# One v transfer cut over Sync and GpSimd, 45 repeated transposes, and three fewer product repeats, in an attention and spectral-mix kernel bound by its weight stream

## The chip, the cores and the metric

One core of one Trainium2 chip. The metric is device time in microseconds (us) of that core; lower is better. The kernel before took 436.51 us (median of 3 runs, 436.29 to 437.32). Every kernel was timed in five rounds against the kernel before on the same chip, and compared by ratios with 95% intervals.

## The reference, cut to what matters

```python
# q, k, v: (8, 8, 576, 64) float32, f: (8, 8, 576)
scores = scale * np.matmul(q, k.transpose(0, 1, 3, 2))
scores = np.where(causal, -1e9, scores + decay)        # decay from cumsum(log f)
attn_out = np.matmul(softmax(scores), v)
x = attn_out.transpose(0, 2, 1, 3).reshape(8, 576, 512)

X = np.fft.rfft(x, axis=1)[:, :64]                     # 64 modes
Yr = einsum('bmd,mde->bme', Xr, w_r) - einsum('bmd,mde->bme', Xi, w_i)
Yi = einsum('bmd,mde->bme', Xr, w_i) + einsum('bmd,mde->bme', Xi, w_r)
y = np.fft.irfft(Y, n=576, axis=1)
u = x + y
out = u + np.maximum(u @ w_ch, 0)
```

The weights w_r and w_i are 64 x 512 x 512 float32 each, 134 MB together. They have to be read once, and this is what most of the time goes to.

## The kernel before

Weights stream through a ring of nine tiles, issued by GpSimd and cast to bf16 on the way; q, k and v of 16 pairs of heads are loaded among them in the same queue. TensorE does attention and multiplies whatever weight tiles have come. After the attention only weight tiles remain, and the last one is handled in four small groups.

```python
    def pool_dma(dst, src):
        keep(nc.gpsimd.dma_start(dst, src))          # program order is kept
    ...
                # loads of pair pr: k, q, v; 128 partitions x 2 x 576 floats
                if nm == "v" and pr < 1:
                    nc.sync.dma_start(dst, ap)
                else:
                    pool_dma(dst, ap)
    ...
        def emit_vback(s):                           # v back to rows, one per step s
            ...
            for sc in range(NSB):                    # five blocks
                nc.tensor.transpose(
                    vp[:, sc, :, :].rearrange("p b d -> p (b d)"),
                    VTs[s // 2 % 2][:, h, sc * 128 : (sc + 1) * 128],
                    ident_bf[:, :],
                )
    ...
        def fill(n):     # products of the tail done again
            for k in range(n):
                rows = slice(k % 2, k % 2 + 1)
                run(*(terms(jobs[0], ps, t, "x")[rows] for t in range(2)), pin=True)

        fill(4)
        emit_modes(nmode)                            # last tile but one
        fill(3)
        emit_modes(nmode + 1, lambda mi, hf: fill((3, 3, 3, 1)[2 * mi + hf]))
```

The softmax here doesn't subtract the row's maximum and nothing guards it: scores larger than these inputs give would overflow.

Of the kernel before, what the change touches and what calls it, by code (L numbers as in the profile page):

```python
# [15 lines left out]
def _strided(ap: bass.AP, free_dims, offset_elems: int = 0) -> bass.AP:  # L16
    new_ap = [list(ap.ap[0])] + [list(x) for x in free_dims]
    return bass.AP(tensor=ap.tensor, offset=ap.offset + offset_elems, ap=new_ap)
# [3 lines left out]
def kernel(  # L22
# [11 lines left out]
    nc = tc.nc  # L34
    B, H, S, Dh = q.shape
# [4 lines left out]
    NSB = 5  # L40
# [14 lines left out]
    NR = S // RP  # L55
    RG = ((0, 5), (5, 4))
    NRING = 9
    STG = 3

    const = ctx.enter_context(tc.tile_pool(name="const", bufs=1))  # L60
    xpool = ctx.enter_context(tc.tile_pool(name="xpool", bufs=1))
# [30 lines left out]
    def pool_dma(dst, src):  # L92
        keep(nc.gpsimd.dma_start(dst, src))  # L93
# [116 lines left out]
    def stage(i):  # L210
        if i != 1:
            return {
                nm: stq.tile(
                    [128, 2, NR, Dh], F32 if nm == "v" else BF16, name=f"st{nm}{i}"
                )
                for nm in "kqv"
            }
        n = 2 * NR * Dh
        flat = {
            "k": wx[:, 0:n],  # L220
            "q": wx[:, n : 2 * n],
            "v": wx[:, 2 * n : 4 * n].bitcast(F32),
        }
        return {
            nm: t.rearrange("p (b r d) -> p b r d", b=2, r=NR)
            for nm, t in flat.items()
        }

    with ExitStack() as actx:
# [25 lines left out]
        NE = 2  # L255
        QKVst = [stage(i) for i in range(STG)]
        VTs = [kt.tile([128, 2, SP], BF16, name=f"VT{i}") for i in range(2)]
# [6 lines left out]
        def emit_loads(pr):  # L264
            dc, bp, _ = steps[2 * pr]
            for nm, src in (("k", k), ("q", q), ("v", v)):
                one = src[2 * bp, 2 * dc, :, :]
                dst = QKVst[pr % STG][nm][:, :, :, :].rearrange("p b r d -> p b (r d)")
                ap = bass.AP(
                    tensor=one.tensor,  # L270
                    offset=one.offset,
                    ap=[[NR * Dh, 128], [H * S * Dh, 2], [1, NR * Dh]],
                )
                if nm == "v" and pr < 1:
                    nc.sync.dma_start(dst, ap)
                else:
                    pool_dma(dst, ap)

# [2 lines left out]
        def emit_transposes(pr, what):  # L281
            dc, bp, _ = steps[2 * pr]
            for which in what:
                st = QKVst[pr % STG][which]
                if which == "q":
# [6 lines left out]
                else:  # L292
# [8 lines left out]
                    )  # L301
                if pr < STG:
                    tc.keep_in_program_order(ins)
# [26 lines left out]
        def scratch(parts, *dims):  # L330
# [13 lines left out]
        ft = ftf[:BH, :]  # L344
        nc.sync.dma_start(ft[:], f.rearrange("b h s -> (b h) s"))
        emit_loads(0)
        nc.gpsimd.memset(trimask[:, :], 1.0)
        nc.gpsimd.affine_select(
# [3 lines left out]
            fill=0.0,  # L352
# [8 lines left out]
            fill=0.0,  # L361
            base=0,
            pattern=[[1, 128]],
            channel_multiplier=-1,
        )
        emit_loads(1)
        emit_w_load(0)
        emit_w_load(1)
# [167 lines left out]
        def emit_vback(s):  # L536
            dc, bp, h = steps[s]
            c0 = 2 * bp * H + 2 * dc + h
            vp = psT.tile([128, NSB, 2, Dh], BF16, tag="tr", name="vp")
            for sc in range(NSB):  # L540
                nc.tensor.transpose(  # L541
                    vp[:, sc, :, :].rearrange("p b d -> p (b d)"),
                    VTs[s // 2 % 2][:, h, sc * 128 : (sc + 1) * 128],
                    ident_bf[:, :],
                )
            va = vap.tile([128, NSB, 2, Dh + 1], BF16, tag="va", name="va")
            nc.vector.tensor_copy(va[:, :, :, 0:Dh], vp[:, :, :, :])
            nc.vector.tensor_copy(
                va[:, :, :, Dh : Dh + 1],
                _strided(wdec[:, 0, c0 : c0 + 1], [[BH, NSB], [H, 2], [1, 1]]),  # L550
            )
            vaugs[s] = va
# [163 lines left out]
        for s in range(NS + 1):  # L716
            pr, h = s // 2, s % 2
            if s == 0:
                emit_loads(STG - 1)
            if h == 1 and pr + STG < NPR:  # L720
                emit_loads(pr + STG)
# [23 lines left out]
            if s < NS:  # L745
                emit_scores(s, 3)
                emit_vback(s)
# [7 lines left out]
    with ExitStack() as bctx:  # L755
# [219 lines left out]
        def terms(job, ps, t, what):  # L975
            rows = [[] for _ in range(2 * len(job))]
            for tt, i, o, hs, src, basis, ysrc in pieces(job):
                if tt != t:
                    continue
                p = ps[t][o, i, :]  # L980
                r = 0 if wide(job) else 2 * i
                rows[r].append((p, ident_bf[hs, hs], src, True))
                rows[r + 1].append((p, basis, ysrc, False))
            return [r for k, r in enumerate(rows) if r and "xy"[k % 2] in what]

        def run(*lists, pin=False):
            for k in range(max(len(l) for l in lists)):
                for l in lists:
                    for a in l[k] if k < len(l) else ():
                        ins = add(*a)  # L990
                        if pin:
                            tc.keep_in_program_order(ins)
# [59 lines left out]
        def fill(n):  # L1052
            for k in range(n):
                rows = slice(k % 2, k % 2 + 1)
                run(*(terms(jobs[0], ps, t, "x")[rows] for t in range(2)), pin=True)

        fill(4)
        emit_modes(nmode)
        fill(3)
        emit_modes(  # L1060
            nmode + 1,
            lambda mi, hf: fill((3, 3, 3, 1)[2 * mi + hf]),
# [83 lines left out]
```

## Time and profile before

| | before |
|---|---|
| time, median | 436.51 us |
| span of the profiled execution | 435.2 us |
| TensorE (PE) busy | 368.1 us, 85% |
| granted TensorE clock, mean | 0.824 |
| last weight landing | 400.19 us |
| from there to the end | 35.0 us |

The page of the kernel before adds two rows, busy tenths over 40 slices of the span:

```profile
PEclk9996899996558665586565869589999999989997
DMA  8999999999999999999999999999999999995797
```

The first is TensorE's granted clock: in the attention stages (from about 100 to 285 us, the 10th to the 26th digit) it is often near one half. The second is the DMA engines: full up to the 36th digit, which ends at 391.7 us; the last weights land in the slice after it.

Several numbers below come from counting the records of the trace rather than from a view. The sorted times of a weight transfer's 16 landings show how far the DMA engines have drifted apart ("stagger"). What bounds a weight tile is the sixteenth.

### The profile page before, as it was taken

How to read it: one execution, taken by the hardware profiler on the slowest of the kernel's cores; microseconds unless marked ns; L12 is line 12 of the kernel's file. 1: busy time of each engine (PE TensorE's matmuls, PEld its weight loads, DVE VectorE, ACT ScalarE, POOL GpSimd, SP SyncE). 2: the span in 40 equal slices, each digit the busy share in tenths (PEclk: the TensorE clock that was granted, in tenths of full speed). 3: DMA queues.
4: the chain of work that ended last, by engine and by line, in shares of the span. 5: the costliest groups of instructions: out<-in, count | busy, mean ns of one | idle time of the engine just before them, and what ended most of it. 6: DMA issues, size and time to landing. Idle time of an engine off the chain costs nothing.

```text
span 435.2 us, 12314 instructions
## 1 busy us (share of the span) xinstructions
PE 368.1 (85%) x5313; PEld 249.7 (57%) x5313; DVE 263.7 (61%) x659; ACT 224.4 (52%) x339; POOL 126.8 (29%) x198
## 2 busy tenths in 40 slices
PE   3787799999987879778787788799999998899881
PEld 2454566776666666566565666656665555454540
DVE  5797888876555655555557568533332665553892
ACT  2887488774526454365462646134434443631781
POOL 8333332333233233232333222223223223200400
PEclk9996899996558665586565869589999999989997
DMA  8999999999999999999999999999999999995797
GB/s 184 234 235 241 234 236 238 235 212 236 234 215 236 225 224 237 210 238 233 214 237 211 212 211 212 211 211 211 211 211 211 212 210 211 211 211 100 253 367 274
DMA packets 50982, 97.38 MB, mean 224 GB/s; under 512 B 3792, under 2 KB 12976, under 8 KB 50928
## 3 DMA queue, kind: packets, MB, share of 16 engines
q0 software_dynamic: 46560, 86.09, 100.9%
q1 hardware_dynamic: 4368, 10.51, 6.7%
q8 instruction: 41, 0.67, 0.6%
q14 instruction: 13, 0.11, 0.1%
HBM read 163.73 MB, written 9.44 MB: 398 GB/s over the span
## 4 chain that ended last, share of the span: by engine, by line
PE 35%; DMA 26%; ACT 12%; DVE 10%; issue 4%; SPq 0%; DVEq 0%; POOL 0%; ACTq 0%
DMA wb<-in_moe_w_i_dram 25%; ACT E L576 8%; PE pav L614 7%; PE ps L569 7%; PE A L188 6%; PE tp L307 5%; PE px L657 2%; PE vp L541 2%; DVE QTs L322 2%; ACT KT L320 2%; ACT VT L326 2%; DVE XT L671 1%; DVE os L1005 1%; DVE E L591 1%; PE px L682 1%
## 5 line engine op out<-in xcount | busy, mean ns | idle before, releaser
L576 ACT ACTIVATE E<-ps 128x1024 bf16<-128x1024 f32 (+1 forms) x128 | 101.5, 851 | 26.1 <-PE ps L569 15.4
L93 POOL DMA_DIRECT2D wb<-in_moe_w_r_dram x64 | 42.5, 664 | 128.9 <-PE A L188 25.1
L188 PE MATMUL A<-XT,wb 128*128 128x16 bf16 x1984 | 69.9, 181 | 8.2 <-DMA wb<-in_moe_w_i_dram 3.8
L188 PEld LDWEIGHTS <-wb 128*128 128x128 bf16 x1984 | 63.5, 100 | 22.8 <-issue 11.9
L569 PE MATMUL ps<-QTs,KT 64*128 64x64 bf16 (+4 forms) x384 | 60.2, 334 | 16.6 <-ACT E L576 14.7
L93 POOL DMA_DIRECT2D wb<-in_moe_w_i_dram x64 | 42.3, 661 | 77.5 <-DMA wb<-in_moe_w_i_dram 32.5
L614 PE MATMUL pav<-va,E 128*128 128x65 bf16 (+1 forms) x1088 | 57.1, 214 | 3.2 <-DVE x_all L636 2.6
L614 PEld LDWEIGHTS <-E 128*128 128x128 bf16 (+1 forms) x1088 | 47.0, 118 | 16.9 <-issue 7.0
L591 DVE TENSOR_TENSOR E<-E,trimask 128x256 bf16<-128x256 bf16 (+2 forms) x128 | 36.9, 303 | 20.0 <-ACT E L576 19.8
L326 ACT COPY VT<-tp 128x640 bf16<-128x640 bf16 (+1 forms) x32 | 23.2, 761 | 33.4 <-PE tp L307 33.4
L867 ACT CAST XW<-pxw 128x512 bf16<-128x512 f32 x36 | 20.7, 586 | 35.9 <-PE pxw L860 28.3
L569 PEld LDWEIGHTS <-KT 64*128 64x128 bf16 x384 | 19.4, 100 | 33.6 <-issue 22.8
L860 PE MATMUL pxw<-wch,yy 128*128 128x512 bf16 x144 | 36.0, 388 | 0.0
L320 ACT COPY KT<-tp 128x640 bf16<-128x640 bf16 (+1 forms) x32 | 21.9, 749 | 26.0 <-PE tp L307 25.8
L910 ACT CAST XW<-pB 128x512 bf16<-128x512 f32 x36 | 21.0, 585 | 25.4 <-PE pB L828 25.3
L909 DVE CAST x_all<-pA 128x512 bf16<-128x512 f32 x36 | 24.9, 692 | 14.2 <-PE pA L828 12.5
L322 DVE COPY QTs<-tp 128x640 bf16<-128x640 bf16 (+1 forms) x32 | 23.4, 767 | 14.3 <-PE tp L307 14.0
L636 DVE TENSOR_TENSOR x_all<-pav,rcp 128x384 bf16<-128x384 f32 x64 | 29.1, 455 | 0.9
L625 DVE RECIPROCAL rcp<-pav 128x6 f32<-128x6 f32 x64 | 12.1, 189 | 25.1 <-PE pav L614 24.3
L828 PEld LDWEIGHTS <-ident_bf 64*64 64x64 bf16 (+1 forms) x348 | 15.7, 108 | 17.9 <-issue 9.3
L153 DVE TENSOR_TENSOR YTe<-A,Yacc 128x128 bf16<-128x128 f32 x16 | 5.9, 367 | 33.3 <-PE A L188 33.3
L541 PE MATMUL vp<-ident_bf,VT 128*128 128x128 bf16 x160 | 18.4, 261 | 4.6 <-DVE QTs L322 3.9
(142 smaller groups left out, 617.4 us busy)
## 6 DMA issues: line engine op xcount, KB each, us to landing
wb<-in_moe_w_r_dram POOLq DMA_DIRECT2D x62, 512.0 KB, 16.7
wb<-in_moe_w_i_dram POOLq DMA_DIRECT2D x62, 512.0 KB, 17.3
stv<-in_v_dram POOLq DMA_DIRECT2D x10, 576.0 KB, 15.2
out_dram<-os SPq DMA_DIRECT2D x10, 512.0 KB, 4.5
stk<-in_k_dram POOLq DMA_DIRECT2D x11, 288.0 KB, 15.3
stq<-in_q_dram POOLq DMA_DIRECT2D x11, 288.0 KB, 15.1
wx<-in_v_dram POOLq DMA_DIRECT2D x5, 576.0 KB, 15.4
out_dram<-uo SPq DMA_DIRECT2D x3, 512.0 KB, 3.6
```

Source lines behind the costliest of these rows:

```text
L93: keep(nc.gpsimd.dma_start(dst, src))
L188: ins = nc.tensor.matmul(A[:, eb, mi, :], lhsT=w_of(mi, eb * 128), rhs=x_of(m), start=(i == 0), stop=(i == len(terms) - 1),)
L320: nc.scalar.copy(rows(KTs[pr % 2][:, :, 0:S]), tv)
L322: ins = nc.vector.tensor_copy(rows(QT[pr][:, :, :]), tv)
L326: nc.scalar.copy(rows(VTs[pr % 2][:, :, 0:S]), tv)
L541: nc.tensor.transpose(vp[:, sc, :, :].rearrange("p b d -> p (b d)"), VTs[s // 2 % 2][:, h, sc * 128 : (sc + 1) * 128], ident_bf[:, :],)
L569: nc.tensor.matmul(ps[:, b, o : o + n], lhsT=KTs[pr % 2][bs, h, jb * 128 : (jb + 1) * 128], rhs=QT[pr][bs, h, jb * 128 + c0 : jb * 128 + c ...
L576: nc.scalar.activation(E[:, :, piece * 512 : piece * 512 + w], ps[:, :, 0:w], ACT.Exp, scale=scale,)
L591: nc.vector.tensor_tensor(dg, dg, tr, ALU.mult)
L614: nc.tensor.matmul(pav[64 * half : 64 * half + w, slot, :], lhsT=E[:, b, c : c + (w - 1) * st + 1 : st], rhs=va[:, jb, b, :], start=(n == ...
L636: nc.vector.tensor_tensor(xo, pi, ri, ALU.mult)
L860: nc.tensor.matmul(pxw[:, :], lhsT=xT[:, eb, i * 128 : (i + 1) * 128], rhs=wch[:, eb, :], start=(eb == 0), stop=(eb == NDC - 1),)
```

## The change

Its stated intent: shift TensorE's instruction fetches by 45 repeated transposes of v, put v of the ninth pair on Sync for 95 partitions, and run fewer product repeats ahead of the last tile.

```diff
+    VREP = range(16, 25)
+    SKEW = (8,)
+    CUTS = (95, 96,)
...
                 if nm == "v" and pr < 1:
                     nc.sync.dma_start(dst, ap)
+                elif nm == "v" and pr in SKEW:
+                    for p0, p1 in zip((0,) + CUTS, CUTS + (128,)):
+                        part = bass.AP(
+                            tensor=one.tensor,
+                            offset=one.offset + p0 * NR * Dh,
+                            ap=[[NR * Dh, p1 - p0], [H * S * Dh, 2], [1, NR * Dh]],
+                        )
+                        if p1 < 128:
+                            nc.sync.dma_start(dst[p0:p1, :, :], part)
+                        else:
+                            pool_dma(dst[p0:p1, :, :], part)
                 else:
                     pool_dma(dst, ap)
...
-            for sc in range(NSB):
+            for sc in [0] * (5 if s in VREP else 0) + list(range(NSB)):
...
-        fill(4)
+        fill(2)
         emit_modes(nmode)
-        fill(3)
+        fill(2)
```

## The prediction

> **What bounds the kernel now.** I read the chain of work that ended last first, then the DMA part of the page, then busy time by stage, then single waits of TensorE near the end. The chain, from 340 us on:
>
> ```profile
> 364.31 20.18 DMA wb<-in_moe_w_i_dram
> 384.49 0.28 issue
> 384.77 15.42 DMA wb<-in_moe_w_i_dram
> 400.19 0.04 issue
> 400.23 0.36 PE A L172 x8
> ...
> 402.17 1.45 PE pu L828 x12
> ```
>
> From 288 to 400 us the chain is weight loads one after another; 40 ns after the last landing at 400.19 the last eight products of a weight tile run, and from there 35.0 us of sums, evictions and stores lead to 435.2. So the end is the last weight landing plus a tail. The queue rows of the page say that this landing is a matter of throughput:
>
> ```profile
> q0 software_dynamic: 46560, 86.09, 100.9%
> q1 hardware_dynamic: 4368, 10.51, 6.7%
> q8 instruction: 41, 0.67, 0.6%
> ```
>
> GpSimd's queue holds the 16 DMA engines busy for the whole span. The 41 packets of q8 are 16 KB each; the trace's packet records show each taking 0.88 to 1.02 us while the stream runs, and they come every 256 TensorE instructions or so: they are TensorE's instruction fetches. They matter because they are uneven. Each transfer's semaphore shows 16 landings, one for each DMA engine. Sorted and taken relative to the first, the last of a weight transfer's 16 comes 1.0 us later at 23 us, 3.1 us at 107 us, 4.2 us at 190 us, 5.3 us at 271 us and 7.74 us for the very last one (first 392.45, eighth 396.43, last 400.19). Each fetch throws one engine back by about 0.5 to 1.1 us, and the packet durations repeat with period 8 (893, 893, 948, 945, 935, 974, 974, 961 ns): the fetches go round 8 of the 16 engines. At the end about 8 engines have lost little (six of them 0 to 0.9 us) and six fetch-laden ones are 6.5 to 7.7 us late. The tile is complete only with the latest.
>
> TensorE is nearly as tight. The stretches (us; then busy time and count for PE, PEld, DVE, ACT, POOL; clock; DMA share; GB/s):
>
> ```profile
> 145.00:170.00 25.00, 21.48 (x305) 15.81 (x304) 14.56 (x40) 12.36 (x18) 7.06 (x11) 0.64 1.13 224
> 195.00:220.00 25.00, 21.28 (x292) 15.82 (x291) 14.79 (x37) 10.94 (x16) 7.52 (x12) 0.57 1.13 222
> 288.00:345.00 57.00, 57.00 (x832) 35.76 (x831) 21.23 (x52) 24.10 (x42) 17.62 (x25) 1.00 1.12 211
> 345.00:385.00 40.00, 36.09 (x480) 20.25 (x478) 22.70 (x43) 19.18 (x33) 10.56 (x17) 0.96 1.12 211
> ```
>
> From 288 to 345 us PE never stops, and later it waits for weights only at 359.06 (0.25 us), 364.06 (1.57), 374.01 (0.15) and 379.82 (1.82), together 3.79 us, and at the very end:
>
> ```profile
> 379.82 0.82 PEld L188 LDWEIGHTS <-wb 128*128 128x128 bf16 x30 [1.92 <-DMA wb<-in_moe_w_i_dram]
> ...
> 400.23 0.27 PEld L172 LDWEIGHTS <-wb 128*128 128x128 bf16 x8 [0.61 <-DMA wb<-in_moe_w_i_dram]
> ```
>
> The other switches of weights beside it show a wait of 0.41 us put down to issue, so the true wait at 400.23 is about 0.2 us: the product repeats are sized to fill the wait almost exactly.
>
> **What the Trainium skill says.** "DMA: Bandwidth & Descriptors", section "Why a DMA increments its semaphore by 16 and not by 1": a transfer runs on the largest k up to 16 that divides both sides' slowest dimension, and from SP on the lowest-numbered k engines. 95 is 5 times 19, so the 95-partition piece should go to engines 0 to 4, 19 partitions each. The trace of before has no such transfer, so this is untested here. The same page, section "Issuing engines are not separate DMA queues": transfers from any engine share the same 16 DMA engines; the 6.7% share of q1 beside q0's 100.9% agrees that Sync has no DMA engines of its own, so moving v to Sync gains only by where it puts bytes. "Runtime: NRT & Kernel Launch", section "Instruction fetch mechanics": instructions come in 16 KiB blocks of 256 by DMA; the 41 packets of 16,384 bytes agree. "TensorE: Matmul & The Clock Gate", Part 1: the clock is halved after idle windows and restored by activity; the clock records here are 0.5 or 1.0 only, 0.57 to 0.72 on average in the attention stages.
>
> **The change part by part.**
>
> *v of the ninth pair.* Before, one 128-partition GpSimd transfer (issued at 86.82, landed 99.17 to 101.35): 128 packets of 4,608 bytes, 181 ns each, 8 on every engine, 1.45 us. Now GpSimd moves 32 partitions, 2 on each engine: every engine saves 6 x 181 = 1.09 us. Engines 0 to 4 get 19 more, so 13 net, +2.36 us (two of them one short row more for the lone partition). If these five are engines without fetches, they stand some 3.45 us nearer to the latest, at 3.5 to 4.4 us against 6.5 to 7.7: still early. The latest engine then ends 1.09 us sooner: last landing at 399.1. That the stagger of the five is worse for a time around 100 us is harmless: TensorE waits for no weights in the attention stages. Sum: -1.09 us on the path.
>
> *Repeated transposes.* Steps 16 to 24 transpose the first block of v five extra times: 45 weight loads and 45 matmuls. Five such transposes take 0.69 us as the chain shows them (PE vp L541 x5), so one is 0.138 us and the 45 are 6.2 us of PE time, all between about 145 and 235 us. The instruction order shows a local reshuffle in those steps and none after. PE is idle some 15 to 20% there behind ScalarE and VectorE, so I expect half to three quarters to show: PE reaches 288 us later by 3 to 4.5 us, less if the extra activity buys full clock. This is off the path as long as PE arrives at the tile of 379.8 before it lands. Without its waits it would arrive at 376.03; with the landing at 378.7 there is room for 2.7 us at no loss, and for about 1.3 us more before the gain is eaten, as the next point adds slack. The load queue is also safe: its thinnest moment, the issue at 279.80, comes 3.24 us before the first engine has ended its last queued packet, and 8.5 us before the latest one has. Sum: 0, at worst +1.
>
> *Fetch places.* PE has 90 more instructions from step 24 on, and 24 fewer after the repeats: 10,593 become 10,659. The fetch at 396.9 moves to about 395.4, those at 405.2 and 416.2 to about 403 and 414 by before's clock. The one of 405.2 stays behind the last tile's wait (some 70 instructions short of it), so the number of fetches before the last landing is the same, 39, and no engine is relieved by it. In the tail it meets other 16 KB row moves and stores; VectorE paces that part. Sum: 0, plus or minus 0.5.
>
> *Fewer repeats.* Three units of four 64x512 products fall away. A unit of three took 0.64 us between two weight groups (397.14 to 397.8 or so), so one is 0.215 us and the three 0.65 us. PE could be at the last weights at about 399.35 instead of 400.0 even if nothing earlier moved; with the earlier tiles also 1.09 us sooner it is there in time for 399.1. It gives nothing itself; without it some of the 1.09 us would be lost to PE. Sum: 0, a condition.
>
> Together -1.09 us, less perhaps 0.1 for what TensorE keeps back: 436.51 - 1.0 = 435.5 us.
>
> **Rivals.** First, engines 0 to 4 may be among the fetch-laden ones. Then their 2.36 us go on top of the latest: last landing about 402.5, 438.9 us. Nothing in the trace names an engine, and this is against it: the cut at 95 makes sense only to someone who knows that the five are early. I give it one in eight. Second, TensorE may become the bound: with 5 us of delay that nothing absorbs, PE's own path ends at 400.0 - 0.65 - 3.79 + 5 = 400.6, 0.3 us later than now: 436.9 us. Against it: a wait of 1.92 us now drops the clock to half from 381.0 to 384.4; if that wait goes, so may this drop, worth up to half of 3.4 us. One in five for losing most of the gain. Third, the clock: extra work might hold it at full rate for more of 155 to 250 us; PE would arrive early and only wait longer for the stream, so 435.4 us, no further gain. Fourth, the tail: the moved fetches might free a store that holds a buffer (the store of 416.86 is on the chain with 3.64 us), up to -1 us: 434.5.
>
> **Range and chances.** The sure gain of 1.09 us is 0.25%; nothing in the parts is near 8.7 us (2%), even the first rival. 8 in 10: 434.2 to 437.0, which holds the tail's gain and the TensorE-bound case but not the engine mix-up. Faster by over 2%: 0.01, within 2%: 0.98, slower: 0.01.
>
> **What would show it.** The last weight landing some 1.1 us sooner, near 399.1, with the 16 landings' stagger about 7.7 - 1.1 or less between the old early engines and the latest, and five engines 3.4 us nearer: right on v. A landing later by 2.4: the first rival. No wait for weights in front of L188 after 345 us and PE busy 100% up to 400: the second. Clock above 0.64 and 0.57 in the two attention stretches shown: the third. A tail other than 35.0 us: the fourth. The prediction is wrong as a whole if the last landing stays at 400.2 while engines 0 to 4 did take their share, since then the latest engine is not bound by bytes.

## The result, and the profile after

| | before | after |
|---|---|---|
| time, median of 6 runs (lowest to highest) | 436.4 (436.16 to 437.32) | 435.89 (435.38 to 436.13) |
| ratio, 95% interval | | 0.9984 (0.9971 to 0.9997) |
| span of the profiled execution | 435.2 | 434.3 |
| granted clock | 0.824 | 0.860 |
| last weight landing | 400.19 | 399.33 |
| from there to the end | 35.0 | 34.95 |
| start of the last attention product | 272.77 | 269.69 |

A ratio is the mean time of one kernel's runs over that of the other's of the same rounds, so it is not quite the ratio of the medians quoted beside it. The kernel after is faster by 0.16%, and the interval just leaves out no change at all.

The chain that ended last, after, from 364 us on (start, duration, what; line numbers are 3 to 14 higher than before):

```profile
364.20 19.62 DMA wb<-in_moe_w_i_dram
383.82 0.28 issue
384.11 15.23 DMA wb<-in_moe_w_i_dram
399.33 0.05 issue
399.38 0.36 PE A L175 x8
...
401.32 1.45 PE pu L842 x12
```

It is the chain of before with one number changed: the last weight transfer lands at 399.33 in place of 400.19. The chain's kind has not changed, nor has the tail.

The DMA queues after (packets, MB, share of 16 engines' span):

```profile
q0 software_dynamic: 46464, 85.65, 101.0%
q1 hardware_dynamic: 4567, 10.95, 7.1%
q8 instruction: 42, 0.69, 0.6%
q14 instruction: 13, 0.11, 0.1%
```

GpSimd's queue has 96 packets less, one of 4,608 bytes for each partition that moved. Sync's has 199 more: by the trace's packet records, 192 of 2,304 bytes and seven of 4 bytes. So a partition that goes by Sync takes two packets of about 106 ns each, 0.21 us together, where GpSimd's queue takes one of 181 ns. The semaphore of the 95-partition transfer shows five landings (86.43 to 87.53 us), the number of engines that the prediction reckoned with (e7 shows one, e8 seven, e10 four); the records don't name the engines.

There is one instruction fetch more, for the 45 repeats, but it comes behind the last weights; before them there are 39 in both kernels. The fetches from 380 us on came at 389.1, 396.9, 405.2 and 416.2 us before, and at 383.1, 393.3, 401.3, 413.4 and 425.1 after: they did move.

TensorE's stretches after (us; busy time and count of PE, PEld, DVE, ACT, POOL; clock; DMA share; GB/s):

```profile
145.00:170.00 25.00, 21.00 (x350) 16.71 (x348) 14.13 (x40) 13.45 (x20) 7.41 (x12) 0.79 1.13 224
195.00:220.00 25.00, 20.13 (x308) 15.51 (x306) 15.15 (x39) 11.23 (x16) 7.27 (x12) 0.69 1.13 222
288.00:345.00 57.00, 55.90 (x810) 35.27 (x820) 22.16 (x53) 24.07 (x42) 16.42 (x23) 1.00 1.12 211
345.00:385.00 40.00, 32.57 (x473) 19.09 (x475) 21.49 (x40) 18.30 (x32) 10.76 (x17) 1.00 1.12 211
```

More TensorE work was added in the first two stretches and yet PE is busy for less of them: the clock is 0.79 and 0.69 where it was 0.64 and 0.57. In the last one PE is busy for 32.57 us where it was 36.09: it has come early and waits for weights. The weight loads ahead of each tile show the same (in brackets the idle time ahead and what ended it):

```profile
349.02 0.81 PEld L191 LDWEIGHTS <-wb 128*128 128x128 bf16 x30 [0.85 <-DMA wb<-in_moe_w_i_dram]
...
363.95 0.81 PEld L191 LDWEIGHTS <-wb 128*128 128x128 bf16 x30 [1.66 <-DMA wb<-in_moe_w_i_dram]
...
378.85 0.82 PEld L191 LDWEIGHTS <-wb 128*128 128x128 bf16 x30 [1.07 <-DMA wb<-in_moe_w_i_dram]
383.86 0.81 PEld L191 LDWEIGHTS <-wb 128*128 128x128 bf16 x30 [1.35 <-DMA wb<-in_moe_w_i_dram]
...
399.38 0.27 PEld L175 LDWEIGHTS <-wb 128*128 128x128 bf16 x8 [0.72 <-DMA wb<-in_moe_w_i_dram]
```

Before, TensorE first waited at 359.06; after, it waits from 349.02 on. So in this profile TensorE came earlier, where the prediction had it later. Whether the repeats did that is asked under e12; kernels without them (e1, e4) also wait from 349 us on in their profiles.

The stagger of the 16 DMA engines, counted from the trace (first landing in us, then each engine's lateness against the first):

```
v load's neighbours, at 88 us
  before  87.38  .00 .07 .11 .18 .33 .46 .57 .63 1.22 1.52 1.57 1.70 1.94 2.12 2.15 2.18
  after   87.90  .00 .14 .28 .81 .84 1.33 1.33 1.37 1.45 1.64 1.73 | 4.04 4.14 4.50 4.55 5.27
the last weights
  before 392.45  .00 .21 .36 .48 .66 .89 2.31 3.98 4.62 4.87 6.49 6.76 6.83 7.05 7.20 7.74
  after  391.92  .00 .26 .82 4.43 4.53 5.27 5.73 5.92 6.18 6.25 6.26 6.35 6.56 6.89 6.91 7.41
```

The five engines right of the bar carry the 95 partitions, 19 each. At the end three engines are early where there were six. The order by rank hides which engine is which, but the very last one can be followed, since it stays alone at the top: 5.27 us late at 88 us, 5.89 at 142, 6.29 at 225, 6.80 at 322 and 7.41 at the end. The latest engine after is one of the five.

Up to 6.80 it climbs in three steps of about 0.5 us. The page has a second instruction queue, q14, with 13 packets of 8 KB, and three of the seven that come between 140 and 390 us (146, 219, 310 us) fall where its steps are, between the last landing without the step and the first with it. The other four (148, 231, 259, 386 us) fall on steps of about 0.3 us of engines just below it. I take these packets to be the other engines' instruction fetches; no record names the DMA engine that they use. The last 0.6 us of the latest engine's climb come after 386 us, when most of the others fall back by 0.4 to 0.8 us too.

### The profile page after: what moved, and what is told of

The parts are those of the page before. It is cut to its first block, busy times and chain, and to the rows that moved or that the text cites. A ratio compares the mean times of both kernels' runs of the same rounds, so it can differ in the third digit from the quotient of the medians. Undisturbed runs are those within 1.5% of the kernel's fastest.

```text
span 434.3 us, 12369 instructions
## 1 busy us (share of the span) xinstructions
PE 358.8 (83%) x5328; PEld 247.5 (57%) x5346; DVE 264.4 (61%) x659; ACT 225.0 (52%) x339; POOL 126.8 (29%) x198
## 4 chain that ended last, share of the span: by engine, by line
PE 33%; DMA 27%; ACT 11%; DVE 11%; issue 5%; DVEq 0%; POOL 0%; ACTq 0%; SPq 0%
DMA wb<-in_moe_w_i_dram 26%; ACT E L590 8%; PE pav L628 7%; PE A L191 6%; PE ps L583 6%; PE tp L321 5%; PE vp L555 3%; PE px L671 2%; DVE QTs L336 2%; ACT KT L334 2%; DVE x_all L650 1%; DVE os L1019 1%; PE pz L842 1%; DVE XT L685 1%; DVE E L605 1%
## 5 line engine op out<-in xcount | busy, mean ns | idle before, releaser
L191 PE MATMUL A<-XT,wb 128*128 128x16 bf16 x1984 | 71.9, 181 | 12.0 <-DMA wb<-in_moe_w_i_dram 7.0
L583 PE MATMUL ps<-QTs,KT 64*128 64x64 bf16 (+4 forms) x384 | 55.8, 320 | 14.5 <-ACT E L590 12.4
L628 PE MATMUL pav<-va,E 128*128 128x65 bf16 (+1 forms) x1088 | 53.6, 205 | 7.1 <-DVE x_all L650 6.5
L628 PEld LDWEIGHTS <-E 128*128 128x128 bf16 (+1 forms) x1088 | 43.6, 111 | 17.2 <-DVE x_all L650 8.9
L881 ACT CAST XW<-pxw 128x512 bf16<-128x512 f32 x36 | 20.7, 587 | 35.6 <-PE pxw L874 23.4
L874 PE MATMUL pxw<-wch,yy 128*128 128x512 bf16 x133 | 33.6, 385 | 1.1 <-issue 0.5
L555 PE MATMUL vp<-ident_bf,VT 128*128 128x128 bf16 x205 | 21.4, 256 | 4.5 <-DVE QTs L336 3.8
```

Of the source, the lines that this page charges most:

```text
L191: ins = nc.tensor.matmul(A[:, eb, mi, :], lhsT=w_of(mi, eb * 128), rhs=x_of(m), start=(i == 0), stop=(i == len(terms) - 1),)
L555: nc.tensor.transpose(vp[:, sc, :, :].rearrange("p b d -> p (b d)"), VTs[s // 2 % 2][:, h, sc * 128 : (sc + 1) * 128], ident_bf[:, :],)
L583: nc.tensor.matmul(ps[:, b, o : o + n], lhsT=KTs[pr % 2][bs, h, jb * 128 : (jb + 1) * 128], rhs=QT[pr][bs, h, jb * 128 + c0 : jb * 128 + c ...
L628: nc.tensor.matmul(pav[64 * half : 64 * half + w, slot, :], lhsT=E[:, b, c : c + (w - 1) * st + 1 : st], rhs=va[:, jb, b, :], start=(n == ...
L874: nc.tensor.matmul(pxw[:, :], lhsT=xT[:, eb, i * 128 : (i + 1) * 128], rhs=wch[:, eb, :], start=(eb == 0), stop=(eb == NDC - 1),)
```

## The experiments

The theory after the result: the v cut alone makes the gain, by taking bytes from the engines that end late; the repeats and the fewer product repeats give nothing. The rivals: the fetch places or the fewer repeats carry a part; or the parts only gain together. A second question was whether the split fits for the reason that the prediction gave. Twelve kernels ran, four to a call; each call has its own runs of the kernel before (medians 436.97, 436.6 and 437.05 us).

### Each part alone

**e1_v_only**: the v cut alone.

```diff
 (against after)
-    VREP = range(16, 25)
+    VREP = range(0)
-        fill(2) ... fill(2)
+        fill(4) ... fill(3)
```

> The kernel before with the ninth pair's v cut as in the change, and nothing else. Byte theory (the last weight landing is set by the engine with most bytes, and v takes 1.09 us off the fetch-laden ones): last landing 0.8 to 1.1 us sooner than 400.19, but the product repeats in front of the last weights keep TensorE until about 400.0, unless the wait at 379.82 lets the whole run of work start sooner too; so 0.2 to 0.9 us less time. Clock theory (the gain comes from the repeated transposes): no gain, 0.0 us, and the clock in the attention stages as before, about 0.64 of full speed.

Measured: 436.05 us (435.33 to 436.71), ratio 0.9979 (0.9964 to 0.9995).

**e2_repeats_only**: the 45 repeated transposes alone (`SKEW = ()`, fills 4 and 3).

> The kernel before with the 45 repeated transposes alone. Clock theory (the extra work keeps TensorE's clock up): half-clock time between 100 and 285 us falls from 132.7 us to about 106 us as in the changed kernel, the attention ends 3 us sooner (269.7 against 272.8), and the time does not move, because the weights still land at 400.2: within 0.3 us. Delay theory of the prediction: attention ends 3 to 4.5 us later. If the sooner TensorE or the moved fetches shorten the time by themselves: 0.5 us or more less.

Measured: 436.99 us (436.26 to 437.29), ratio 0.9998 (0.9984 to 1.0013).

**e3_fills_only**: the fewer product repeats alone (`VREP = range(0)`, `SKEW = ()`).

> The kernel before with fewer product repeats alone. Byte theory: TensorE waits some 0.6 us longer for the last weights, landing at 400.2, and the time is the same within 0.2 us. Rival (TensorE, not the landing, set the end): up to 0.6 us less. A further rival: the fetch places alone (24 instructions) move the tail, by up to 0.5 us either way.

Measured: 436.78 us (436.25 to 437.23), ratio 0.9995 (0.9979 to 1.0011).

**e4_no_repeats**: the kernel after without the repeated transposes (`VREP = range(0)`).

> The changed kernel without the repeated transposes. Byte theory: as the changed kernel, last landing near 399.3, 0.6 us less than before, within 0.2 us of the changed kernel (435.9). Clock theory: the gain is gone, and TensorE arrives later in the weight stages, so 436.4.

Measured: 435.96 us (435.44 to 436.37), ratio 0.9977 (0.9963 to 0.9992).

**e5_no_v**: the complement of e1, the kernel after without the v cut (`SKEW = ()`).

> The changed kernel with v of the ninth pair back as one GpSimd transfer; the repeated transposes and the fewer product repeats stay. It is the complement of the run with the v cut alone. Theory that the v cut is the whole gain: ratio to the kernel before 1.000 plus or minus 0.0015, last weight landing at 399.9 to 400.3. Rival, that the three parts only gain together or that the repeats carry a part: 0.9985 or less. Rival, that repeats and fewer fills cost something that the v cut hides: 1.002 or more.

Measured: 437.12 us (436.78 to 438.0), ratio 0.9997 (0.9978 to 1.0016).

What follows: with the v cut, with or without the other parts, the ratio is 0.9977 to 0.9984; without it, with any of the others, it is 0.9995 to 0.9998. The v cut is worth 0.16 to 0.23%, 0.7 to 1.0 us, and it is the whole gain that these runs resolve. The other parts have no effect of more than about 0.2% either way.

One expectation missed. In e5's profile the last weights landed at 399.46, which is as early as with the cut, and its span is still 435.1: the tail took 35.6 us. Its chain shows where, with a small transfer in it that the chains of before and after go round:

```profile
399.46 0.04 issue
399.51 0.36 PE A L175 x8
...
403.02 2.11 DMA yy<-yl
```

Last landing and tail move from one profile to the next by as much as the effect: among the five kernels that put v evenly on the engines (before, e2, e3, e5, e9) the landing goes from 399.46 to 400.58 us, and the tail goes from 33.8 us (e1) to 35.6 (e5). The landing of a single profile cannot carry 0.2%; the rounds do.

Over these profiles the mean landing with the cut (after, e1, e4, e12) is 399.70 us and without it 400.05, 0.35 us apart, while the mean spans are 0.95 us apart. So the rounds show that the cut gains; that all of the gain comes by the earlier landing is not shown by the profiles.

### Where the bytes are put

**e9_all_sync**: all 128 partitions of that v by one Sync transfer, so evenly on 16 engines.

```diff
 (against after)
-    CUTS = (95, 96,)
+    CUTS = ()
-                        if p1 < 128:
+                        if p1 <= 128:
```

> The changed kernel with the whole of the ninth pair's v in one 128-partition Sync transfer, so spread over all 16 engines. Byte theory: no engine is relieved, last landing near 400.0, time as before within 0.3 us. Rival (moving v off GpSimd's queue is what helps, wherever its bytes go): the gain of the changed kernel, 0.5 to 0.9 us, remains or grows.

Measured: 436.94 us (436.38 to 437.4), ratio 1.0005 (0.9992 to 1.0019).

So it is not the move from GpSimd to Sync as such that gains, but the uneven split.

**e6_two_pairs**: the same cut for two pairs (`SKEW = (8, 11)`).

> The changed kernel with the same cut of v at the ninth and the twelfth pair. If more bytes off the fetch-laden engines always helps: last landing about 1.1 us sooner than the changed kernel's 399.3, time 434.9. Byte theory with the five engines as the new latest (in the changed kernel one engine that had taken the Sync bytes is already the last, at 7.41 us of stagger): that engine gets 2.4 us more, last landing about 401.5, time 437.5 to 438.3, later than before.

Measured: 438.99 us (437.96 to 439.28), ratio 1.0048 (1.0034 to 1.0062). Its chain:

```profile
387.99 15.20 DMA wb<-in_moe_w_i_dram
403.19 0.05 issue
403.24 0.36 PE A L175 x8
```

The last landing is 403.19, 1.7 us later than expected, with the fifteenth at 400.52: one engine alone is 2.7 us behind the rest. At 88 us, after the first cut load, the stagger ends in 3.62, 3.86, 3.97, 4.49, 6.04; at 133 us, after the second, in 7.41, 7.62, 7.87, 8.36, 9.83. Each of the five has moved by 3.8 to 3.9 us (7.41 less 3.62, 9.83 less 6.04), 19 partitions at 0.2 us, and not at the 0.181 us that was expected. So both loads fell on the same five engines, and one load fits what they have in hand where two do not. With the five clear of the rest, this trace also shows what the packets of q14 do: those at 146, 219 and 313 us fall on steps of the latest engine, those at 148 and 260 us on steps of the next of the five (8.36 to 8.71 us late, then 7.06 to 7.37), and the one at 235 us on a step of another (6.0 to 6.25). The remaining two of the five show no step between 160 and 380 us.

**e7_engine0**: 31 partitions and 1 by Sync, 96 by GpSimd (`CUTS = (31, 32,)`).

> The changed kernel with 31 partitions of the ninth pair's v in one Sync transfer, a prime, so that all of it should fall on one engine, one more partition on Sync, and 96 partitions (6 for each engine) on GpSimd. One engine gets about 29 x 181 ns = 5.25 us more and stands out in the stagger; all others 0.36 us less. If it is free of all fetches (392.5 to 393.4 before): it ends at about 398, last landing 399.8, time 0.2 to 0.4 less than before. If it takes the 8 KB fetches of the other engines' queues (394.8 or 396.4 before): last landing 400 to 401.7, same as before or up to 1.5 us more. If it takes TensorE's fetches: 404 and up, 4 us more.

Measured: 436.35 us (435.73 to 436.51), ratio 0.999 (0.9975 to 1.0004). One engine stands out by 6.44 us at 88 us, and it stays at about 6.4 to 6.5 until 300 us, while the others come up to it one by one. It takes no fetch of any kind in that time: this engine is free of them.

**e8_119**: 119 partitions by Sync, 17 on each of seven engines, 9 by GpSimd (`CUTS = (119,)`).

> The changed kernel with 119 of the ninth pair's 128 partitions on Sync (7 times 17, so seven engines with 17 each) and 9 on GpSimd. Byte theory, engines 5 and 6 free of TensorE's fetches too: seven engines get 9 to 10 partitions more (1.7 us, not 2.36), the others 7 to 8 less (1.3 to 1.45 us, not 1.09): last landing 398.6 to 399.0, time 0.3 to 0.6 us less than the changed kernel. If engine 5 or 6 takes TensorE's fetches: last landing 401.5 or later, time 1.3 us or more above before.

Measured: 439.29 us (438.65 to 440.65), ratio 1.0062 (1.0046 to 1.0078). Its chain:

```profile
386.57 15.43 DMA wb<-in_moe_w_i_dram
402.04 0.36 PE A L175 x8
```

Two engines climb here that did not before: at 206 us the top two are 7.07 and 7.43 us late, then about 8.1 and 8.5, and from 362 us on 9.25 and 9.60, with 7.66 for the third. Their last two climbs come at the fetches of 275.4 and 283.7 us and again at those of 354.0 and 364.5, which are the eighth after them. So two of e8's seven engines take TensorE's fetches, each once in eight. If the seven are the five and two more, as the rule that the prediction quotes has it, five is where the engines without them end.

**e10_four**: 76 partitions on four engines and 4 more on the same four, 48 by GpSimd (`CUTS = (76, 80,)`).

> The cut at 76 and 80 in place of 95 and 96: 76 partitions by Sync on four engines (19 each), 4 more by Sync (one each on the same four), 48 by GpSimd (3 on each engine). The other engines save 5 rows of 181 ns, 0.91 us instead of 1.09; four engines take 15 net rows (2.7 us) and the fifth engine none. If the fifth of the five is the one that ended latest in the changed kernel, the last landing comes at about 399.2 (all other engines 0.18 us later than there, the second latest then at 398.83) and the ratio is 0.997 to 0.998. If it is one of the first four, that one is 0.36 us later than in the changed kernel: last landing about 399.7, ratio 0.9985 to 1.000.

Measured: 436.51 us (436.23 to 436.76), ratio 0.998 (0.9963 to 0.9997). Four engines jump, to 4.43, 4.60, 5.00 and 5.86 us at 87 us, and the one at the top climbs in the same small steps, 6.38, 6.70, 7.21, and is at 7.86 us at the end. So the climbing engine is among the first four, as the rival had it, and not the fifth; the landing, at 399.95, is on that side too (399.7 expected). By the rule that the prediction quotes e7 loads the first engine, which takes nothing; whether the climbing one is the second, third or fourth stays open. The ratio lies in the range expected for the fifth engine (0.997 to 0.998) and not in the one for the first four (0.9985 to 1.000), but its interval holds both; the trace decides here, not the time.

**e11_85**: 85 partitions on the five engines, 11 on eleven (`CUTS = (85, 96,)`).

> The cut at 85 and 96: 85 partitions on five engines (17 each), 11 by Sync on eleven engines (one each), 32 by GpSimd. The five take 18 rows instead of 19 or 20, so the one of them that ended latest in the changed kernel stands 0.18 to 0.36 us better; six of the eleven others take one row more (0.18 us). Theory that the cut at 95 overshoots on one of the five: last landing 399.0 to 399.2, ratio 0.9970 to 0.9980, at best 0.3 us under the changed kernel. Rival, that the latest engine's end is a matter of where fetches happen to fall: no ordering beyond noise, 0.9975 to 0.999.

Measured: 437.1 us (436.18 to 438.2), ratio 0.9992 (0.997 to 1.0014). This is the one that should have beaten the kernel after, and did not; its interval holds no change and the gain of the kernel after alike, and the rival that was named for it, the chance places of fetches, is not ruled out. Its one profile shows two things against it, neither foreseen. The first landing (which the lighter load hardly touches) was already 1.0 us later than after's at 88 us (88.90 against 87.90); one profile doesn't tell why. And the chain at the end no longer runs over the last weights:

```profile
365.38 19.60 DMA wb<-in_moe_w_i_dram
384.98 0.05 issue
385.02 0.91 PE A L191 x30
...
387.19 0.43 PE pA L842 x2
387.62 0.43 PE pB L842 x2
...
394.58 0.22 PE pB L842 x2
...
401.05 0.29 PE A L175 x8
```

From 385 us on it is all TensorE. The pairs of products take 0.43 us each at first and 0.22 later: from 386.5 to 389.9 the clock records have TensorE at half rate. That costs half of 3.4 us, and so the last products come at 401.05, 0.77 us behind the landing at 400.28. The stretches of e11 show the clock (eighth figure, behind the five engines):

```profile
385.00:388.00 3.00, 2.98 (x44) 1.89 (x46) 1.06 (x2) 0.58 (x1) 0.53 (x1) 0.75 1.11 209
388.00:392.00 4.00, 4.00 (x48) 2.00 (x45) 1.71 (x3) 1.61 (x3) 0.00 (x0) 0.76 1.12 210
```

The profiles of e4 and e10 have the same window (from 385.3 and 385.9 us) and the same end: last products at 400.23 and 400.48, 0.5 us behind their landings. The profiles of after, e1 and e12 have no such window there; that of before has one at 381.0 to 384.4 us, over before the last tiles. This is the prediction's second rival, TensorE as the bound, for 0.5 to 0.8 us and only in some executions. All the kernels but before wait for weights between 384 and 388 us, most of them for 1.3 us (2.8 us in e9), and only these three have a drop there, so the wait alone doesn't explain it.

### How much the repeats delay TensorE

**e12_20_repeats**: 20 extra transposes in each of the nine steps instead of 5.

```diff
 (against after)
-            for sc in [0] * (5 if s in VREP else 0) + list(range(NSB)):
+            for sc in [0] * (20 if s in VREP else 0) + list(range(NSB)):
```

> The changed kernel with 20 extra transposes in each of the nine steps instead of 5: 180 of them, at 0.138 us 24.8 us of TensorE time, 18.6 us more than in the changed kernel. My predicted step, that half to three quarters of this shows as a later end of the attention stages: the last attention product ends 9 to 14 us later than in the changed kernel (269.7), which uses up the waits for weights near the end (some 7 us) and moves the end by 2 to 8 us, ratio 1.002 to 1.017. Rival, that repeats fill idle time or buy full clock and so cost nothing: last attention product within 4 us of 269.7, ratio 0.9970 to 0.9990, mean clock higher.

Measured: 437.03 us (435.48 to 437.71), ratio 0.9987 (0.9964 to 1.0009). The stretch from 100 to 285 us of before, of after and of e12, one line each:

```profile
100.00:285.00 185.00, 154.67 (x2287) 115.48 (x2284) 110.62 (x300) 86.00 (x130) 54.40 (x81) 0.64 1.13 222
```

```profile
100.00:285.00 185.00, 151.80 (x2371) 115.69 (x2369) 111.54 (x301) 87.99 (x133) 56.75 (x85) 0.71 1.13 222
```

```profile
100.00:285.00 185.00, 155.44 (x2481) 123.55 (x2481) 111.33 (x300) 87.94 (x132) 55.68 (x83) 0.75 1.13 221
```

The matmul count rises from 2,287 to 2,371 to 2,481, the busy time hardly at all, and the clock from 0.64 to 0.71 to 0.75. The last attention product started at 274.46, 4.8 us later than after's: a quarter of the 18.6 us of added work, not the half to three quarters of my step.

That share is rough, since this time moves a lot between profiles: 267.1 to 272.8 us in the four kernels without repeats (mean 270.1), 264.6 to 272.7 in the nine with five per step (mean 267.5). Against that mean e12 is 7.0 us later, 38% of the added work. At the end it cost nothing that these runs resolve, as TensorE still waited for weights at 364 to 385 us. The stream was touched, though: in e12's trace no load is issued from 272.81 to 281.49 us, and the first engine's next landing comes 3.48 us after the one before it where 2.48 is usual, so it stood idle for 1.0 us.

Is it the repeats that raise the clock? A single profile can't say, since the mean clock of the kernel before itself goes from 0.827 to 0.872 in the eleven runs of the first call. The means over all runs of a kernel can be set side by side:

```
mean granted clock over all runs     without repeats                    with repeats
first call    before .852, e1 .851, e3 .845, e4 .849                    e2 .864
second call   before .851                    e6 .858, e7 .871, e8 .854, e9 .857
third call    before .850                    e5 .868, e10 .870, e11 .874, e12 .863
```

All nine kernels with repeats have a higher mean than their call's kernel before, by 0.003 to 0.024, and in the first call than every kernel without; the kernel after had 0.869 in its own runs. The fourfold dose is no higher than the single one. By this it is likely that the repeats raise the clock a little; a mechanism was not isolated.

No version was found that beats the kernel after: e1, e4 and e10 are as fast within the intervals.

## Why the prediction was right or wrong, point by point

**The bound** was right. After the change the chain is still weight landings and then a tail of 34.95 us, which the prediction put at 35.0.

**The v cut, -1.09 us on the path**, was right in kind and near in size: the landing moved by 0.86 us between the profiles of before and after (by 0.35 us in the mean of more profiles, see e5), and the runs give 0.7 to 1.0 us. Part of the nearness may be luck: the size was reckoned for engines that are no longer the last. e1 shows that it acts alone, e9 that it needs the uneven split, e6 that twice as much is too much.

What failed in this step is a part: "these five ... stand ... at 3.5 to 4.4 us against 6.5 to 7.7: still early". Four of the five stood at 4.04 to 4.55 us at 88 us, a little above; the fifth was at 5.27 and ended as the very latest, since it climbs by 1.5 us in small steps that go with the packets of q14, a queue which I had left out of the account although the page lists it. The reading that about 8 engines had lost little was loose for the same reason: before, only six ended within 0.9 us of the first, and the next two at 2.31 and 3.98. The cost of a partition was mis-sized too: I took 181 ns, GpSimd's, for those on Sync, where two packets take some 0.21 us. With that, 19 of them less the 1.09 us saved are +2.9 us where I had +2.36, and the five stand 4.0 us nearer to the latest and not 3.45; e6 measured 3.8. The latest engine ends 0.5 us behind the next in the profile after (399.33 against 398.83), 0.55 us in e1 and 0.40 in e4. Whether sparing it would win that 0.5 us was not shown: e10 and e11 did not isolate it.

**The first rival, that engines 0 to 4 are laden with TensorE's fetches**, was rightly held unlikely: the landing came earlier, not 2.4 us later. e8 shows what that would have looked like, two engines further on.

**The repeated transposes: "PE reaches 288 us later by 3 to 4.5 us"** was wrong. The attention ended 3.1 us earlier in the profile after, and 2.7 us earlier in the mean of the nine profiles with the repeats than in the four without. The step failed by its fraction: I took half to three quarters of the added time as delay at a fixed clock. e12 measured a quarter, or 38% against the mean, for a dose that is four times as large, at a clock that was higher. I had named this possibility, "less if the extra activity buys full clock", and as the third rival, but weighed it as an afterthought. It cost the predicted time nothing because the sum had rightly put TensorE's arrival off the path.

**Fetch places, 0 plus or minus 0.5**: right in the sum. The fetches ahead of and in the tail came 2.8 to 3.9 us earlier rather than the 1.5 to 2.2 predicted, as TensorE was early, and the number ahead of the last landing stayed 39. e2, which has the shift and not the cut, is at 0.9998. So shifting the fetches did not show in the time, though it is in the change's name.

**Fewer product repeats, "a condition"**: wrong as a condition. e1 keeps all of them and gains 0.21%; in its profile TensorE came earlier than I had it. They remain a margin for executions with a half-clock window such as those of e4, e10 and e11, in which TensorE was the bound in spite of them; no run here shows what the margin is worth.

**The second rival** did not come in the profile after, but it is real in other executions (e4, e10, e11), through a half-rate window and not through the added transposes.

**The fourth rival, the tail**: unchanged in the profile after. Between profiles it went from 33.8 us (e1) to 35.6 (e5), 1.2 us below to 0.6 us above the 35.0, with no tie to a part of the change that I could show.

## What to carry to other kernels

When a stream is bound by the latest of 16 DMA engines, look at the stagger of the landings of one transfer, not only at the queue's share: the same bytes placed on early engines gained 0.2%, placed evenly they gained nothing that shows, and twice as many lost 0.5%. Before loading an engine that looks early, check what else it has to carry, and count every instruction queue. And when the gain looked for is a few tenths of a per cent, let five rounds decide: one profile's landing and tail each wander by as much.

## What the Trainium skill lacked or had wrong

- "Runtime: NRT & Kernel Launch", "Instruction fetch mechanics", calls the cost of a 16 KiB boundary mostly hidden. For the fetching engine that may be so; for a saturated weight stream it is not. In the trace of before each of TensorE's 39 fetches ahead of the last landing held a DMA engine for 0.88 to 1.02 us, their durations repeat with period 8, and after them the 16 engines were 7.7 us apart. e8 showed the round directly: the same two engines were hit again at the eighth fetch after.
- No page tells which DMA engines carry instruction fetches. Here the five that the 95-partition transfer uses took none of TensorE's; the latest of them climbed by 1.5 us (5.27 to 6.80) in three steps that go with 8 KB packets of q14, two more climbed in steps of about 0.3 us, and two showed no step (e6).
- No page says that an uneven transfer can be used to balance such engines: 19 partitions of 4.6 KB put each of five engines 3.8 us later in e6.
- "TensorE: Matmul & The Clock Gate", Part 1, has the clock drop after at least one idle window of about 3.4 us. The drops near the end last 3.4 us, which agrees, but they came after waits of 1.3 us, with TensorE busy for 63 to 65% of the 3.4 us before (e4, e10, e11), and most profiles with the same wait had none; in e9 it was busy for 50% of such a stretch (381.3 to 384.7 us) and no drop followed.
- The same page, Part 4, says that transposes in transpose mode don't count as busy in the same way and don't engage the full clock. The trace doesn't name the mode of these transposes; adding 45 (180 in e12) went with a mean clock of 0.864 over nine kernels, against 0.850 in the runs without, so the page is not shown to be wrong.
